# Windowed attention and a spectral filter on one core: query and key stacks kept threefold in DRAM, and the score maxima passed through DRAM

## The chip, the cores and the metric

The program runs on one core of one Trainium2 chip. The metric is the time on the device of one execution, in microseconds (us). The kernel before takes 1365.38 us, the median of three runs from 1363.18 to 1367.34. The profile is of one execution with a span of 1361.8 us between its first and its last instruction; the 3.6 us up to the median lie outside that span.

## What is computed

The input `x` has 2048 tokens of 576 features. Four steps follow one another, attention (A), spectral filter (B), A, B, each added to its input after a layer norm. The attention has 32 heads of 18 features and a window of 256 tokens.

```python
def _A_ref(x, wqkv, wo):                       # S = 2048, D = 576
    H = 32; Dh = D // H; W = 256
    qkv = transpose((x @ wqkv).reshape(B, S, 3, H, Dh), 2, 0, 3, 1, 4)
    q, k, v = qkv[0], qkv[1], qkv[2]
    scores = einsum("bhqd,bhkd->bhqk", q, k) * (Dh ** -0.5)
    mask = (idx[:, None] - idx[None, :] >= 0) & (idx[:, None] - idx[None, :] < W)
    p = softmax(where(mask, scores, -1e9))
    return transpose(einsum("bhqk,bhkd->bhqd", p, v), 0, 2, 1, 3).reshape(B, S, D) @ wo

x = x + _A_ref(_layernorm(x), A_wqkv, A_wo)
x = x + _B_ref(_layernorm(x), B_w_r, B_w_i)    # rfft2, times a weight, irfft2
x = x + _A_ref(_layernorm(x), A_wqkv, A_wo)
x = x + _B_ref(_layernorm(x), B_w_r, B_w_i)
```

## The kernel before

All the work around the change is in `layer_a`, which runs twice, once for each attention. The order of the instructions is written out by hand, and each engine and each queue of DMAs keeps the order of the program.

**Numbers in two parts.** TensorE multiplies in a reduced float format, so a float is kept as a high part and a low part, and a product is made of high times high, high times low and low times high. For a score of queries and keys this is one matmul over a stack of rows: the query stack has the features' high parts, their high parts again, and their low parts; the key stack has high, low, high. One head has 18 features, so that a stack is 54 rows. `qs` and `ks` (two buffers each) hold the stacks of one group `n` of four heads: head half `hp` 0 in partitions 0 to 53 and `hp` 1 in partitions 64 to 117, two heads (`pair`) side by side in the columns. There are NQ = 8 groups. Partition 63 (and 127) of `qs` holds minus the maximum of each query's scores, and the same partition of `ks` holds ones, so that the second score matmul subtracts the maximum.

**Projection.** `proj(i, c)` makes 128 columns of queries and keys (block `i` of 9) for a chunk `c` of 512 tokens, with 14 matmuls (L1112). ScalarE takes the high part (L1124), VectorE the low part (L1127, in `remainder`), and one DMA writes both to `qk_d` in DRAM (L1129, 512 KB): `qk_d[part, column, token]`. For blocks 0 and 1 it goes out on ScalarE's queue, for the others on SyncE's (SP). `qk_cols` sets the order of the columns: all the queries of group 0, then its keys, then group 1.

**Stacks.** `stack_load(n, c)` reads `qk_d` back. A row of 18 features with one part goes to its own 18 partitions, so a chunk of a group takes 2 (queries, keys) x 2 (`hp`) x 3 (slots of the stack) = 12 DMAs of 72 KB (L1144), nearly all on SP.

**Two score matmuls and the maxima.** `score_max` multiplies queries by keys (L1169) and takes each query's maximum (L1171) into a tile `ms[n, c]`. `m_rows(n, c)` transposes that tile (L1182), ScalarE copies it with a minus sign to `mt`, 16 rows of 128 (L1184), and four DMAs of 2 KB move it within the SBUF to row 63 or 127 of `qs` (L1189), on SP (for the first two chunks on ScalarE's queue). `exps` multiplies keys by queries with that row (L1206) and takes the exponential (L1207). `part` multiplies by the values (L1226), `norm` transposes the sums, divides and stores to `o_d` (L1251, on SP).

**The order.** `x` counts tiles of 128 tokens, 16 in each group. `opening` runs ten steps of score maxima (LEAD = 10) beside projections. `bursts` then runs 158 bursts `k`, each with three `exps` and three `score_max`, some `part`, one or two tasks out of `due` (`m_rows` or `norm`) and a few matmuls of `pj`, the projections still to be made. At the start of a burst `loads(x)` issues the stack loads (every fourth `x`, 20 tiles ahead) and the loads of values (`v_load`, once for each group, beside chunk 2 of the same group's stack). A store of a projection that ended in a burst is issued by `remainders()` in the next burst. The first `exps` that reads chunk `c` of a group is that of tile 4c-2 (tile 0 for chunk 0). Two short loops follow for the tiles from MIX = 118.

Of the kernel before, what the change touches and what calls it, by code (L numbers as in the profile page):

```python
# [632 lines left out]
NQ = 8  # L633
# [13 lines left out]
def qk_cols():  # L647
    c = []
    for n in range(NQ):
        for qk in range(2):  # L650
            for hp in range(2):
                for pair in range(2):
                    h = head_of(n, hp, pair)
                    c += [qk * D + h * DH + d for d in range(DH)]
    return np.array(c)
# [209 lines left out]
def layer_a(tc, ident, eps, bp, src, dst, wqk_d, wv_d, wo_d, dc_d, gc_d, dram, copy, wvs, second, spectral, share):  # L865
# [4 lines left out]
    qk_d = dram.tile([2, 1152, S], F32R, name="qk_d")  # L870
# [12 lines left out]
    if True:  # L883
# [192 lines left out]
        with ExitStack() as c2:  # L1076
# [21 lines left out]
            def proj(i, c, bank=0):  # L1098
# [5 lines left out]
                def mm(s, k):  # L1104
# [8 lines left out]
                    if s == len(ks) - 1:  # L1113
                        if 4 * i + c < 12:

                            sg = wp.tile([128, 4, 384], F32, tag="P", name=f"sg{i}_{c}", bufs=6)
                            sg = sg.rearrange("r a b -> r (a b)")[:, 0:1024].rearrange("r (a t) -> r a t", a=2).bitcast(F32R)
                        else:
                            sg = wp.tile([128, 2, 512], F32R, tag="sg", name=f"sg{i}_{c}", bufs=2)
                        by, rest = box["ps"], sg  # L1120
                        if second:
                            by = by.rearrange("r (n p) -> r p n", n=NT)
                            rest = sg.rearrange("r a (p n) -> r a p n", n=NT)
                        A.copy(rest[:, 0], by)  # L1124

                        def remainder():
                            V.tensor_sub(rest[:, 1], by, rest[:, 0].bitcast(F32))  # L1127

                            (nc.scalar if i < 2 else nc.sync).dma_start(qk_d[:, 128 * i:128 * i + 128, cs].rearrange("a r t -> r a t").bitcast(F32), sg.bitcast(F32))  # L1129
                        ended.append(remainder)  # L1130
# [4 lines left out]
            def stack_load(n, c):  # L1135
# [3 lines left out]
                for which, t, parts in ((0, q, (0, 0, 1)), (1, k, (0, 1, 0))):  # L1139
                    for hp in range(2):  # L1140
                        r0 = 144 * n + 72 * which + 36 * hp
                        for slot, part in enumerate(parts):
                            b = 64 * hp + 18 * slot
                            (P if which and (n == 0 and c > 1 or n == 1 and c == 0) else nc.sync).dma_start(  # L1144
                                t[b:b + 18, :, cs].bitcast(F32), qk_d[part, r0:r0 + 36, cs].rearrange("(f d) t -> d f t", f=2).bitcast(F32))
# [33 lines left out]
            def m_rows(n, c):  # L1179
# [5 lines left out]
                for hp in range(2):  # L1185
                    for pair in range(2):
                        r = (hp * 2 + pair) * 4
                        b = 64 * hp + 63
                        (nc.sync if n or c > 1 else nc.scalar).dma_start(q[b:b + 1, pair, c * 512:c * 512 + 512].rearrange("a (t q) -> a t q", t=4).bitcast(F32),  # L1189
                                          mt[r:r + 4].bitcast(F32))  # L1190
# [75 lines left out]
            done, due = 0, []  # L1266
# [16 lines left out]
            def opening():  # L1283

                n = 0
                for t in range(-LEAD, 0):
# [8 lines left out]
                    if y > 0 and y % 4 == 3:  # L1295
                        m_rows(0, y // 4)
                    yield from pj[n + 3:want]
# [12 lines left out]
            def bursts():  # L1310
# [8 lines left out]
                for k in range(-(-len(es) // 3)):  # L1319
# [40 lines left out]
                    for f, *a in tasks:  # L1360
                        f(*a)
                    for f in pj[at + early:at + n]:
# [6 lines left out]
                    due.extend(new)  # L1369
                    for x, pair, hp in e:  # L1370
# [55 lines left out]
            for t in range(MIX, NX + 2):  # L1426
# [9 lines left out]
                if MIX < y < NX - 1 and y % 4 == 3 and t != NX - 1:  # L1436
                    due.append((norm, *divmod(y // 4, 4)))
                for f, *a in due[:1]:
                    f(*a, *([True] if f is norm else []))
                    due.pop(0)  # L1440
                behind(t)
            assert not due
# [76 lines left out]
```

## Time and profile before

| what | value |
|---|---|
| time of the kernel, median of 3 runs | 1365.38 us (1363.18 to 1367.34) |
| profiled execution, span | 1361.8 us |
| busy: VectorE, ScalarE, GpSimd | 900.8, 779.3, 642.9 us |
| attention in bursts, first layer and second layer | about 128 to 443 us and 822 to 1141 us |
| read from HBM, written to HBM | 156.11 MB, 101.01 MB |

Times in the profile count from the first instruction. PE is TensorE's matmul, PEld its load of weights, DVE VectorE, ACT ScalarE, POOL GpSimd, SP SyncE, which only issues DMAs here; a q behind an engine's name is its sequencer, so that SPq L1144 is the issue of a DMA by line 1144. An issue's duration is the time for which it holds its queue, not the transfer's. `qs<-mt` is an instruction that reads `mt` and writes `qs`. A busy PE is not PE at its peak: matmuls are pipelined.

### The profile page before, as it was taken

The numbers are of one execution on the slowest core, as the hardware profiler recorded it, in microseconds if no ns is written. First come the engines' busy times: TensorE is split into PE (matmuls) and PEld (weight loads), VectorE is DVE, ScalarE is ACT, GpSimd is POOL, SyncE is SP. The second block draws the span as 40 slices with busy tenths as digits, with TensorE's granted clock in tenths as the row PEclk, the third lists the DMA queues.
The fourth block names the chain that finished last, engine by engine and source line by source line (L and its number), as shares of the span: only waits on it lengthen the run. The fifth ranks groups of instructions, "written<-read, shape, count | busy, mean of one in ns | idle before, by whom it ended". The sixth has DMA issues, their size and how long they took to land.

```text
span 1361.8 us, 33597 instructions
## 1 busy us (share of the span) xinstructions
PE 1333.3 (98%) x11351; PEld 994.7 (73%) x11351; DVE 900.8 (66%) x3060; ACT 779.3 (57%) x1966; POOL 642.9 (47%) x1154
## 2 busy tenths in 40 slices
PE   9999999999999999999999999999999999999998
PEld 8986666666665699975999975566666655898587
DVE  5418777877778366666673157777777785575755
ACT  5522777777778544543355316677777778464223
POOL 2257545555546533477221394445455458112721
PEclk9999999999999999999999999999999999999999
DMA  6756665655546547778873467566555555597875
GB/s 204 208 166 195 206 184 171 192 166 159 153 144 178 134 150 253 225 231 255 268 248 73 113 196 218 167 178 164 165 140 152 159 162 164 143 358 248 309 237 173
DMA packets 202313, 259.11 MB, mean 190 GB/s; under 512 B 104487, under 2 KB 109863, under 8 KB 201631
## 3 DMA queue, kind: packets, MB, share of 16 engines
q1 hardware_dynamic: 191439, 235.72, 57.6%
q10 hardware_dynamic: 7648, 14.96, 3.2%
q0 software_dynamic: 3056, 6.28, 1.8%
q8 instruction: 92, 1.51, 0.5%
q14 instruction: 78, 0.64, 0.1%
HBM read 156.11 MB, written 101.01 MB: 189 GB/s over the span
## 4 chain that ended last, share of the span: by engine, by line
PE 87%; DMA 5%; DVE 3%; issue 2%; ACT 2%; SPq 1%; POOL 0%; ACTq 0%; DVEq 0%; POOLq 0%
PE pj L1112 18%; PE S L1169 12%; PE U L1226 12%; PE vps L1005 8%; PE ops L800 7%; PE E L1206 6%; PE po L257 4%; PE pq L517 2%; PE p L496 2%; PE pf L257 2%; PE tpo L1240 2%; PE pi L591 2%; PE pz L295 2%; DMA qs<-mt 1%; PE tpm L1182 1%
## 5 line engine op out<-in xcount | busy, mean ns | idle before, releaser
L1171 DVE CUSTOM_DVE_ANT_0 jk<-S,mask 128x384 bf16<-128x384 f32 (+2 forms) x1024 | 490.7, 529 | 111.0 <-PE E L1206 53.7
L1207 ACT ACTIVATE P<-E 128x384 f32<-128x384 f32 (+2 forms) x1024 | 408.9, 477 | 125.6 <-PE E L1206 92.1
L1209 POOL TENSOR_SCALAR_AFFINE_SELECT P<-P 128x512 f32<-128x512 f32 x256 | 162.5, 635 | 275.7 <-ACT P L1207 257.3
L1169 PE MATMUL S<-ks,qs 63*128 63x384 f32 (+2 forms) x1024 | 269.5, 371 | 1.1 <-DVE m L1171 0.4
L1206 PE MATMUL E<-qs,ks 64*128 64x384 f32 (+2 forms) x1024 | 222.7, 372 | 4.5 <-ACT P L1207 2.7
L1169 PEld LDWEIGHTS S<-ks,qs 63*128 63x128 f32 x1024 | 140.7, 184 | 105.4 <-DVE m L1171 72.0
L1226 PE MATMUL U<-P,vq 128*19 128x128 f32 (+1 forms) x3840 | 187.8, 328 | 0.6
L1112 PE MATMUL pj<-xh,wqh 128*128 128x512 f32 x360 | 155.9, 433 | 1.5 <-DVE sg L1127 1.1
L1226 PEld LDWEIGHTS U<-P,vq 128*19 128x19 f32 x3840 | 95.9, 98 | 77.1 <-issue 24.3
L1212 POOL TENSOR_SCALAR_AFFINE_SELECT P<-P 128x512 f32<-128x512 f32 x224 | 142.2, 635 | 0.0
L1206 PEld LDWEIGHTS E<-qs,ks 64*128 64x128 f32 x1024 | 113.9, 185 | 19.7 <-ACT P L1207 9.9
L1112 PE MATMUL pj<-xh,wql 128*128 128x512 f32 x360 | 124.4, 419 | 0.0
L1112 PE MATMUL pj<-xl,wqh 128*128 128x512 f32 x288 | 122.1, 424 | 0.0
L800 PE MATMUL ops<-oroom 128*128 128x290 f32 (+1 forms) x812 | 115.4, 298 | 0.4 <-DVE ofree L846 0.2
L800 PEld LDWEIGHTS ops<-oroom 128*128 128x128 f32 x812 | 110.3, 189 | 1.1 <-DVE ofree L823 0.7
L1112 PEld LDWEIGHTS pj<-xh,wqh 128*128 128x128 f32 x360 | 67.7, 188 | 32.3 <-issue 10.6
L1171 DVE DVE_READ_ACCUMULATOR2_ANT m<- 128x1 f32 x1024 | 85.0, 83 | 0.0
L1127 DVE TENSOR_TENSOR sg<-pj,sg 128x512 fp32r<-128x512 f32 x72 | 49.5, 687 | 52.2 <-ACT sg L1124 52.2
L1124 ACT CAST sg<-pj 128x512 fp32r<-128x512 f32 x72 | 42.2, 586 | 68.8 <-PE pj L1112 51.7
L1112 PEld LDWEIGHTS pj<-xh,wql 128*128 128x128 f32 x360 | 64.3, 189 | 20.2 <-issue 10.7
L1005 PE MATMUL vps<-wvh,xh 128*128 128x288 f32 x320 | 71.4, 304 | 0.0
L1112 PEld LDWEIGHTS pj<-xl,wqh 128*128 128x128 f32 x288 | 54.3, 189 | 18.2 <-issue 11.5
(599 smaller groups left out, 2251.9 us busy)
## 6 DMA issues: line engine op xcount, KB each, us to landing
qk_d<-sg SPq DMA_DIRECT2D x56, 512.0 KB
qs<-qk_d SPq DMA_DIRECT2D x384, 72.0 KB
ks<-qk_d SPq DMA_DIRECT2D x348, 72.0 KB
v_d<-vt SPq DMA_DIRECT2D x32, 304.0 KB
vq<-v_d SPq DMA_DIRECT2D x16, 608.0 KB
wt<-in_w SPq DMA_DIRECT2D x16, 580.0 KB
ofree<-x SPq DMA_DIRECT2D x16, 580.0 KB
x<-ofree SPq DMA_DIRECT2D x32, 290.0 KB
```

What stands on the lines that cost most here:

```text
L257: T.matmul(ps[:, c, 0:NF], tail[r] if si == 4 else hl_(si), dcs[b // 2][r, b % 2], start=mi == si == 0, stop=si == 4)
L800: self.nc.tensor.matmul(self.ps[u][n][:, 0:self.n], x, self.w[p][:, (2 * wk + n) * self.n:(2 * wk + n + 1) * self.n], start=first and i == ...
L1005: T.matmul(ps[:, n, 0:288], xT(xk, c), w[:, wk, n * 288:(n + 1) * 288], start=i == 0, stop=i == len(ks) - 1)
L1112: T.matmul(box["ps"].rearrange("r (n p) -> r n p", n=NT) if second else box["ps"], w[:, wk], x, start=s == 0, stop=s == len(ks) - 1)
L1127: V.tensor_sub(rest[:, 1], by, rest[:, 0].bitcast(F32))
L1169: T.matmul(ps[:, 0:N], q[b:b + 63, pair, i * 128:i * 128 + 128], k[b:b + 63, pair, lo:hi], start=True, stop=True)
L1171: V.tensor_tensor_reduce(out=jk[:, 0:N], in0=ps[:, 0:N], in1=mask[:, 384 - N:384], scale=1.0, scalar=-3e38, op0=ALU.add, op1=ALU.max, accu ...
L1206: T.matmul(ps[:, 0:nq], k[b:b + 64, pair, j * 128:j * 128 + 128], q[b:b + 64, pair, j * 128:j * 128 + nq], start=True, stop=True)
L1207: A.activation(p[:, hl_, 0:nq], ps[:, 0:nq], AF.Exp, scale=SC)
L1209: P.affine_select(out=p[:, :, 0:128], in_=p[:, :, 0:128], pattern=[[0, 4], [1, 128]], compare_op=ALU.is_ge, fill=0.0, base=0, channel_mult ...
L1212: P.affine_select(out=p[:, :, 256:384], in_=p[:, :, 256:384], pattern=[[0, 4], [-1, 128]], compare_op=ALU.is_gt, fill=0.0, base=0, channel ...
L1226: T.matmul(U[32 * h:32 * h + 19, (q0 % 4) * 128:(q0 % 4) * 128 + 128 * (q1 - q0)], vts[n][:, j, h], pt[n, j][:, h, (q0 - j) * 128:(q1 - j) ...
```

## The change

Each feature gets three rows in DRAM, in the order in which a stack wants them. `qk_d` becomes `[2, 576, 3, S]`: queries or keys, feature, slot, token. `qk_cols` now puts 64 queries and 64 keys of the same features into each block of 128. A projection's store becomes four DMAs: for queries the high part to slots 0 and 1 (one DMA that reads it twice, 256 KB) and the low part to slot 2 (128 KB), for keys the high part to slots 0 and 2 and the low part to slot 1. A stack of one head half is then 54 rows that lie side by side in DRAM, and a chunk of a group takes 4 DMAs of 216 KB. The 54 partitions now go feature by feature with the slots inside, instead of slot by slot; the matmul sums over them all the same.

The maxima go through a new DRAM tile `m_d`: `m_rows` writes `mt` to it with one DMA of 8 KB, and a new function `m_load` reads it into both rows of `qs` with one more. `m_load` runs at the end of the burst that is two after that of `m_rows` (in the opening one step later, in the last loop one tile later). Both use the queue that the four DMAs had.

```diff
@@ -645,14 +645,8 @@
     return 4 * n + 2 * hp + pair
 
 def qk_cols():
-    c = []
-    for n in range(NQ):
-        for qk in range(2):
-            for hp in range(2):
-                for pair in range(2):
-                    h = head_of(n, hp, pair)
-                    c += [qk * D + h * DH + d for d in range(DH)]
-    return np.array(c)
+    c = np.array([head_of(n, hp, pair) * DH + d for n in range(NQ) for hp in range(2) for pair in range(2) for d in range(DH)])
+    return np.stack([c, D + c]).reshape(2, 9, 64).transpose(1, 0, 2).reshape(-1)
 
 def lay_qkv(wqkv):
     w3 = lay_w3(wqkv[:, qk_cols()])
@@ -867,7 +861,8 @@
     nc = tc.nc
     V, A, T, P = nc.vector, nc.scalar, nc.tensor, nc.gpsimd
     SC = float(DH) ** -0.5
-    qk_d = dram.tile([2, 1152, S], F32R, name="qk_d")
+    qk_d = dram.tile([2, D, 3, S], F32R, name="qk_d")
+    m_d = dram.tile([NQ, 4, 16, 128], F32R, name="m_d")
     v_d = dram.tile([NQ, S, 76] if second else [NQ, 128, NT, 76], F32, name="v_d")
 
     o_d = dram.tile([S, 448], F32, name="o_d")
@@ -1126,7 +1121,12 @@
                         def remainder():
                             V.tensor_sub(rest[:, 1], by, rest[:, 0].bitcast(F32))
 
-                            (nc.scalar if i < 2 else nc.sync).dma_start(qk_d[:, 128 * i:128 * i + 128, cs].rearrange("a r t -> r a t").bitcast(F32), sg.bitcast(F32))
+                            e = nc.scalar if i < 2 else nc.sync
+                            for which, high, low in ((0, slice(0, 2), 2), (1, slice(0, 3, 2), 1)):
+                                d = qk_d[which, 64 * i:64 * i + 64].bitcast(F32)
+                                s = sg[64 * which:64 * which + 64].bitcast(F32)
+                                e.dma_start(d[:, high, cs], s[:, 0:1].to_broadcast([64, 2, 512]))
+                                e.dma_start(d[:, low, cs], s[:, 1])
                         ended.append(remainder)
                 return [lambda s=s, k=k: mm(s, k) for s, k in enumerate(ks)]
 
@@ -1136,13 +1136,11 @@
 
                 q, k = qs[n % 2], ks_[n % 2]
                 cs = slice(c * 512, c * 512 + 512)
-                for which, t, parts in ((0, q, (0, 0, 1)), (1, k, (0, 1, 0))):
+                for which, t in ((0, q), (1, k)):
                     for hp in range(2):
-                        r0 = 144 * n + 72 * which + 36 * hp
-                        for slot, part in enumerate(parts):
-                            b = 64 * hp + 18 * slot
-                            (P if which and (n == 0 and c > 1 or n == 1 and c == 0) else nc.sync).dma_start(
-                                t[b:b + 18, :, cs].bitcast(F32), qk_d[part, r0:r0 + 36, cs].rearrange("(f d) t -> d f t", f=2).bitcast(F32))
+                        r0 = 72 * n + 36 * hp
+                        (P if which and (n == 0 and c > 1 or n == 1 and c == 0) else nc.sync).dma_start(
+                            t[64 * hp:64 * hp + 54, :, cs].bitcast(F32), qk_d[which, r0:r0 + 36, :, cs].rearrange("(a d) s t -> (d s) a t", a=2).bitcast(F32))
 
             def v_load(n):
                 v = wp.tile([128, NT, 4, 19], F32, tag="vq", name=f"vq{n}", bufs=2)
@@ -1182,12 +1180,13 @@
                 T.transpose(tp[0:16, 0], ms[n, c].rearrange("p a b t -> p (a b t)"), ident)
                 mt = wp.tile([16, 128], F32R, tag="mt", name=f"mt{n}_{c}", bufs=2)
                 A.activation(mt, tp[0:16, 0], AF.Copy, scale=-1.0)
-                for hp in range(2):
-                    for pair in range(2):
-                        r = (hp * 2 + pair) * 4
-                        b = 64 * hp + 63
-                        (nc.sync if n or c > 1 else nc.scalar).dma_start(q[b:b + 1, pair, c * 512:c * 512 + 512].rearrange("a (t q) -> a t q", t=4).bitcast(F32),
-                                          mt[r:r + 4].bitcast(F32))
+                m_queue(n, c).dma_start(m_d[n, c].bitcast(F32), mt.bitcast(F32))
+
+            def m_queue(n, c):
+                return nc.sync if n or c > 1 else nc.scalar
+
+            def m_load(n, c):
+                m_queue(n, c).dma_start(qs[n % 2][63:128:64, :, c * 512:c * 512 + 512].bitcast(F32), m_d[n, c].rearrange("(a p t) q -> a p (t q)", a=2, p=2).bitcast(F32))
 
             pt = {}
 
@@ -1263,7 +1262,7 @@
             NX = NQ * NT
             LEAD = 10
             pj = [f for i in range(2, 9) for c in range(4) for f in proj(i, c, c % 2 if i == 2 else c == 0 and i == 3)]
-            done, due = 0, []
+            done, due, steps = 0, [], {}
 
             MIX = 118
 
@@ -1294,6 +1293,8 @@
                     yield from pj[n:n + 3]
                     if y > 0 and y % 4 == 3:
                         m_rows(0, y // 4)
+                    if y > 0 and y % 4 == 0:
+                        m_load(0, y // 4 - 1)
                     yield from pj[n + 3:want]
                     n = want
 
@@ -1359,6 +1360,8 @@
                         yield f
                     for f, *a in tasks:
                         f(*a)
+                        if f is m_rows:
+                            steps.setdefault(k + 2, []).append((m_load, *a))
                     for f in pj[at + early:at + n]:
                         yield f
                     at += n
@@ -1367,6 +1370,8 @@
                     if (3 * k) // 4 + LEAD - 1 < full and full % 4 == 3:
                         new.append((m_rows, *divmod(full // 4, 4)))
                     due.extend(new)
+                    for f, *a in steps.pop(k, ()):
+                        f(*a)
                     for x, pair, hp in e:
                         if pair == hp == 1:
                             behind(x)
@@ -1435,11 +1440,15 @@
                 y = t - 3 if t == NX - 2 else t - 4
                 if MIX < y < NX - 1 and y % 4 == 3 and t != NX - 1:
                     due.append((norm, *divmod(y // 4, 4)))
+                for f, *a in [z for k in sorted(steps) for z in steps.pop(k)]:
+                    f(*a)
                 for f, *a in due[:1]:
                     f(*a, *([True] if f is norm else []))
                     due.pop(0)
+                    if f is m_rows:
+                        steps.setdefault(0, []).append((m_load, *a))
                 behind(t)
-            assert not due
+            assert not due and not steps
             def bank(tag, name):
                 return pp.tile([128, 512], F32, tag=tag, name=name, bufs=1 if tag == "pj" else 3)
 
```

## The prediction

> **What bounds the kernel now.** I read the page first, then TensorE's waits, the DMA issues by line, SP's own queue in order of time, and the chain.
>
> ```profile
> PE 1333.3 (98%) x11351; PEld 994.7 (73%) x11351; DVE 900.8 (66%) x3060; ACT 779.3 (57%) x1966; POOL 642.9 (47%) x1154
> q1 hardware_dynamic: 191439, 235.72, 57.6%
> PE 87%; DMA 5%; DVE 3%; issue 2%; ACT 2%; SPq 1%; POOL 0%; ACTq 0%; DVEq 0%; POOLq 0%
> ```
>
> TensorE is busy 98% of the span and holds 87% of the chain, so a wait costs time where TensorE itself waits. The list of its waits says how much of that DMAs cause:
>
> ```profile
> PE E L1206 <- ACT P L1207: 2.7, 7, 0.5
> ...
> PE E L1206 <- DMA qs<-mt: 1.8, 2, 1.5
> ...
> PE S L1169 <- DMA qs<-qk_d: 0.3, 1, 0.3
> ```
>
> Columns: us in total, times, longest. Only 2.1 us of the whole run hang on the DMAs that the change touches. So nothing much can be won by making them quicker; what counts is whether one of them becomes late. The nearest to that are the maxima. The PE rows that follow are the first `exps` of chunk 1 of group 1 and of chunk 2 of group 2, the ACT rows the ends of their `m_rows`, the DMA rows the chain:
>
> ```profile
> 169.68 0.27 ACT L1184 ACTIVATE mt<-tpm 16x128 fp32r<-16x128 f32 x1
> 178.34 0.93 PE L1206 MATMUL E<-qs,ks 64*128 64x384 f32 x3 [0.30 <-DMA qs<-mt]
> 225.54 0.25 ACT L1184 ACTIVATE mt<-tpm 16x128 fp32r<-16x128 f32 x1
> 231.66 0.62 PE L1206 MATMUL E<-qs,ks 64*128 64x384 f32 x3
> 125.91 2.33 DMA qs<-mt
> 174.34 3.87 DMA qs<-mt
> 870.10 4.26 DMA qs<-mt
> ```
>
> From the end of `mt` (169.95) to the matmul that needs it are 8.4 us, of which 0.3 are already a wait: a budget of 8.1 us, where five bursts lie between. For the other chunk (225.79; the matmul is the third of its three, at about 231.9) four bursts lie between, 6.1 us. A small DMA lands 2.33 us after its issue when little is ahead of it, and 3.87 or 4.26 us where it stands behind other loads. SP's queue shows what stands there:
>
> ```profile
> 162.45 2.28 SPq L1144 DMA_DIRECT2D qs<-qk_d  x6
> 164.78 2.56 SPq L1144 DMA_DIRECT2D ks<-qk_d  x6
> 167.44 2.81 SPq L1144 DMA_DIRECT2D qs<-qk_d  x6
> 170.32 2.23 SPq L1144 DMA_DIRECT2D ks<-qk_d  x6
> 172.65 0.38 SPq L1129 DMA_DIRECT2D qk_d<-sg  x1
> 173.35 0.38 SPq L1251 DMA_DIRECT2D o_d<-o  x1
> 174.34 2.48 SPq L1189 DMA_DIRECT2D qs<-mt  x4
> ```
>
> `mt` was ready at 169.95, its first DMA went out at 174.34 behind two sets of stack loads, and TensorE waited at 178.34. In the second layer the same place (870.10) costs TensorE 1.5 us. That is a late maximum's price: TensorE stands still, for its queue keeps order.
>
> **What goes.** The issues by line (columns: ns min/median/max, first and last start):
>
> ```profile
> L1144 SPq DMA_DIRECT2D qs<-qk_d x384: 265/321/770, 89.6 to 1115.7; - x192
> L1144 SPq DMA_DIRECT2D ks<-qk_d x348: 264/320/1312, 93.7 to 1118.1; - x174
> L1144 POOL DMA_DIRECT2D ks<-qk_d x36: 577/587/808, 114.5 to 823.7; - x36
> L1189 SPq DMA_DIRECT2D qs<-mt x240: 572/573/2832, 138.6 to 1145.8; - x120
> L1129 SPq DMA_DIRECT2D qk_d<-sg x56: 360/387/2451, 124.6 to 1111.0; - x56
> L1129 ACTq DMA_DIRECT2D qk_d<-sg x16: 366/366/397, 84.4 to 799.3; - x16
> ```
>
> Stack loads on SP fall from 732 to 244 (488 x 0.32 = 156 us of SP's time), on POOL from 36 to 12 (24 x 0.59 = 14 us). The maxima's 240 SP issues of 0.573 become 120 of 0.3 to 0.57: 69 to 100 us less. Stores grow from 56 to 224 on SP (168 x 0.387 = 65 us more) and from 16 to 64 on ACT (48 x 0.366 = 18 us more). SP gains 160 to 190 us, and its backlog of 4.4 us (169.95 to 174.34) should vanish. None of it is on the path except the 2.1 us above. The price if that cover is gone is the next part.
>
> **What comes, away from the maxima.** The rows are ACT's copies of two blocks in turn, its issues for chunk 1's maxima, and the last chunk of group 7:
>
> ```profile
> 87.92 0.59 ACT L1124 CAST sg<-pj 128x512 fp32r<-128x512 f32 x1 [2.50 <-PE pj L1112]
> 91.09 0.59 ACT L1124 CAST sg<-pj 128x512 fp32r<-128x512 f32 x1 [2.58 <-PE pj L1112]
> 125.29 2.50 ACTq L1189 DMA_DIRECT2D qs<-mt  x4
> 445.96 0.25 ACT L1184 ACTIVATE mt<-tpm 16x128 fp32r<-16x128 f32 x1
> 449.89 0.90 PE L1206 MATMUL E<-qs,ks 64*128 64x384 f32 x4
> ```
>
> Each store writes 768 instead of 512 KB: 72 x 0.26 = 19 MB more beside 259. In the blocks ahead of the opening ACT issues 4 x 0.37 = 1.5 us for each; a block comes every 3.2 us and ACT's copy takes 0.6, so it fits. In the opening `m_load` waits on ACT's queue until `m_d` has landed, with ACT's copy of the last projection and the first exponentials behind it. Before, four issues held ACT there for 2.5 us, about as long; between 0 and 1.5 us for each layer, I take 0.5. In the last loop the chunk has 3.7 to 4.0 us (446.21 to a matmul of the group at 449.89); two landings of 2.3 make it about 0.5 late in each layer. In return the opening's loads come sooner; I take 1 us off for each layer, up to 1.5.
>
> **What comes, for the maxima.** One transfer becomes two, with a wait of SP between. Two idle landings (4.7 us) fit both budgets. But `m_load` stands at the end of a burst at whose beginning `loads` has issued that period's whole set of stack loads, and often a store and the values, all behind `m_rows` and ahead of `m_load` on SP. Before, the four DMAs of `mt` went out ahead of them. This period shows it:
>
> ```profile
> 225.82 2.53 SPq L1189 DMA_DIRECT2D qs<-mt  x4
> 228.45 0.39 SPq L1129 DMA_DIRECT2D qk_d<-sg  x1
> 228.94 2.47 SPq L1144 DMA_DIRECT2D qs<-qk_d  x6
> 231.45 4.21 SPq L1144 DMA_DIRECT2D ks<-qk_d  x6
> 235.76 0.77 SPq L1152 DMA_DIRECT2D vq<-v_d  x1
> 227.40 0.69 DVE L1127 TENSOR_TENSOR sg<-pj,sg 128x512 fp32r<-128x512 f32 x1
> ```
>
> After the change the order is `m_d`, store (ready at 228.09, when VectorE is done: 2.3 us behind `mt`), four stack loads, values, `m_load`, and the matmul wants it at 231.9. Packets ahead on a queue hold a small DMA up, as 3.87 and 4.26 against 2.33 show, so I let `m_load` wait for all of them.
>
> How long each takes to drain. A set of stack loads: the 24 loads from 162.45 to 172.55 took 10.1 us, 5.05 for twelve, an upper end, since issue may have held them; by q1's row (57.6% of 16 x 1361.8 us for 235.72 MB is 53.2 us for one MB on one engine) 0.885 MB over sixteen engines take 2.9, the lower end. I take 4.3: near the set that was seen, less something for eight DMAs fewer. A store of 0.786 MB over sixteen engines: 2.6 (at the least the 1.7 of today's 0.524 MB). Values, 0.623 MB: 2.0, at the least 1.0.
>
> The Trainium skill speaks here against the change: by "DMA: Bandwidth & Descriptors", section "Why a DMA increments its semaphore by 16 and not by 1", a DMA runs on the largest number of engines up to 16 that divides its outermost dimension, 9 for 18 rows and again 9 for 54, so the wider load is spread no wider. No view here shows the number of engines. With its 27 GiB/s for an engine, an estimate from that page's figure, set, store and values would drain in 3.4, 1.7 and 1.3 us, and the sum below would be 53 us instead of 107.
>
> The order written in `bursts` gives four kinds among the 20 chunks of a layer whose `m_load` has a set ahead of it and whose budget is 6.1 or 8.1 (chunk 0 of each group has over two bursts more and stays in time). 2.3 is the landing of `m_load` itself:
> - set alone (0.4 for the issue of `m_d` + 4.3 + 2.3 = 7.0): late by 0.9 at three chunks of four bursts, in time at four of five: 2.7.
> - set and values (9.0): 0.9 at two, 2.9 at one: 4.7.
> - store and set (2.3 + 2.6 + 4.3 + 2.3 = 11.5): 3.4 at five, 5.4 at one: 22.4.
> - store, set and values (13.5): 5.4 at three, 7.4 at one: 23.6.
>
> That is 53.4 for a layer, 107 for both. TensorE has few other waits that a standstill could absorb, so I count all of it. With the 2.1 us that go, 1 + 1 that come and 2 that the openings give back: 107 - 2 = 105. On the profiled execution's 1361.8 this is 1467; the median of the runs lies 3.6 above that span: **1470 us**. With the lower drains the kinds give 0, 0.5, 8.6 and 10.4, so 39 and 1402; with 5.05 for a set 5.0, 7.0, 26.9 and 26.6, so 131 and 1494.
>
> **The rivals.**
> - *The relief of SP decides* (faster). If `m_load` lands within its budget everywhere, the 2.1 us go and the openings give up to 3: about 1361. It decides once store and set drain within 8.1 - 2.3 - 2.3 = 3.5 us, half of what I sum. The skill's same page, section "Rules for kernel authors", advises to merge many small transfers into a large one; by that rule this is the outcome, and the 160 us of SP's time agree, but TensorE's waits do not need them.
> - *The small load is not held* (no change). Then only issues count: with a store 2.3 + 4 x 0.39 + 4 x 0.33 + 2.3 = 7.5, late at the two chunks of four bursts by 1.4 and 1.8, so 6 for both layers against 4 to 5 given back: 1367. Against it stand 3.87 and 4.26.
> - *Held, but the drains are shorter than my lower ends*, as the engines overlap reads and writes: 1374 to 1402.
> - *The store's parts wait for one another*, because slots 0 and 2 lie around slot 1: SP would stand for a landing of a store, 4.88 in the chain's row below, at ten chunks of a layer: 98 more, 1568.
>
> ```profile
> 830.71 4.88 DMA qk_d<-sg
> ```
>
> **How the numbers follow.** Forecast 0.62 (its own range 1402 to 1494), shorter drains 0.15, between 1494 and 1512 0.03, the store's waits 0.05, no change 0.08, faster 0.07. The range from 1374 to 1512 holds 0.80. Slower by over 0.3% (4 us, about what a measurement of this kernel can tell from no change): 0.85; within 0.3%: 0.08; faster: 0.07.
>
> **What would show it.** TensorE's waits should list L1206 waiting for the DMA of `qs<-m_d` some thirty times, 3 us each, in both layers, longest where store, set and values meet (chunk 2 of groups 0, 2, 4 and 6); SP's queue should have `m_load` right behind four loads of 216 KB; issues on SP should fall by 440. I am wrong if L1206's wait stays under 10 us in total, if `m_load` lands some 2.3 us after its issue behind a set, or if SP stands at the second DMA of a store.

## The result and the profile after

The changed kernel takes 1619.3 us (median of four runs, 1617.37 to 1623.9) against 1366.1 for the kernel before on the same chip: a ratio of 1.186, 95% interval 1.183 to 1.188. That is slower, as forecast, but the forecast loss was 105 us, the measured one 253, and the time lies outside the range. The profiled execution has a span of 1617.9 us, 256.1 more than before.

From the page of the changed kernel come the busy times, the granted clock in 40 slices and the chain by engine:

```profile
PE 1417.3 (88%) x11351; PEld 1045.1 (65%) x11351; DVE 904.1 (56%) x3060; ACT 787.2 (49%) x1966; POOL 631.6 (39%) x1130
...
PEclk9989788799899899999999988987897998999999
...
PE 61%; DMA 25%; SPq 4%; DVE 3%; issue 3%; ACT 2%; POOL 1%; ACTq 0%; DVEq 0%; POOLq 0%
```

TensorE does the same 11351 matmuls and is busy 84.0 us longer with them (1417.3 against 1333.3). Outside them it stands 200.6 us (1617.9 - 1417.3) against 28.5: 172.1 more. So a third of the loss is not waiting at all. DMAs now hold 25% of the chain, against 5%. Its waits (us in total, times, longest) say what it stands for:

```profile
PE E L1205 <- DMA qs<-m_d: 157.5, 34, 8.7
PE E L1205 <- ACT P L1206: 9.8, 6, 4.3
PE pj L1107 <- DVE sg L1122: 9.2, 8, 2.6
```

Thirty-four waits for the maxima's load, 4.6 us each, are 157.5 of the 172.1. Here is one of them, chunk 2 of group 0. First SP's queue, then TensorE, then the chain's row for the load:

```profile
150.31 0.33 SPq L1183 DMA_DIRECT2D m_d<-mt  x1
150.93 0.59 SPq L1128 DMA_DIRECT2D qk_d<-sg  x1
152.84 0.45 SPq L1129 DMA_DIRECT2D qk_d<-sg  x1
153.34 1.49 SPq L1128 DMA_DIRECT2D qk_d<-sg  x1
154.89 0.60 SPq L1129 DMA_DIRECT2D qk_d<-sg  x1
155.53 1.29 SPq L1142 DMA_DIRECT2D qs<-qk_d  x2
156.87 0.76 SPq L1142 DMA_DIRECT2D ks<-qk_d  x2
157.67 0.72 SPq L1150 DMA_DIRECT2D vq<-v_d  x1
158.43 0.61 SPq L1189 DMA_DIRECT2D qs<-m_d  x1
```

```profile
158.47 0.32 PE L1167 MATMUL S<-ks,qs 63*128 63x128 f32 x1
166.84 0.98 PE L1205 MATMUL E<-qs,ks 64*128 64x384 f32 x3 [8.05 <-DMA qs<-m_d]
```

```profile
158.43 8.28 DMA qs<-m_d
```

`m_d` goes out at once. Then come four store DMAs (the second, a low part, waits for VectorE until 152.84), four stack loads and the values; `m_load` is issued 8.1 us after `mt` and lands 8.3 us after that. TensorE stands 8.05 us. What happens to its clock is seen in windows around that wait (window, its length, PE busy and matmuls, PEld, DVE, ACT, POOL, granted clock, DMA share, GB/s):

```profile
150.00:158.00 8.00, 7.86 (x76) 4.82 (x78) 6.68 (x26) 6.32 (x16) 4.77 (x7) 1.00 0.50 112
158.50:166.80 8.30, 0.29 (x5) 0.15 (x1) 0.30 (x2) 0.58 (x1) 1.10 (x2) 0.74 0.82 198
166.80:174.00 7.20, 7.16 (x54) 4.37 (x54) 2.48 (x12) 3.54 (x9) 1.22 (x2) 0.59 0.20 46
174.00:179.80 5.80, 5.80 (x59) 3.65 (x57) 4.34 (x19) 4.20 (x11) 3.11 (x5) 1.00 0.73 168
```

After the wait the clock is at 0.59 for 7 us and TensorE, fully busy, makes 54 matmuls where it made 76 in 8 us before it; then the clock is 1.00 again. The trace has 39 stretches of half clock, 239 us in all, each 3.4, 6.8 or 10.2 us long, against one at the very end before. TensorE is busy for 177 us of them. Outside them its matmuls take as long as in the kernel before (`exps` of 384 columns 382 ns in both kernels on average, projections 423 against 425); those that touch them take 604 and 672. So the longer matmuls are the lower clock's. The Trainium skill, "TensorE: Matmul & The Clock Gate", section "HAM oscillation — how this bites in real kernels", says that a wait for a DMA that fills an activity window of some 3.4 us halves the array's clock and that the next work starts slow. The trace agrees, in steps of 3.4 us.

By stages (between the starts of the first projection of the loop, of the first `exps` and of that of tile 118, both layers): blocks and opening grew by 9.7 and 8.9 us, the bursts by 121.0 and 117.2, everything else together by -0.7.

### The profile page after: what moved, and what is told of

Its sections match the earlier page's. It is cut to its first block, busy times and chain, and to the rows that moved or that the text cites. A ratio compares the mean times of both kernels' runs of the same rounds, so it can differ in the third digit from the quotient of the medians.

```text
span 1617.9 us, 33055 instructions
## 1 busy us (share of the span) xinstructions
PE 1417.3 (88%) x11351; PEld 1045.1 (65%) x11351; DVE 904.1 (56%) x3060; ACT 787.2 (49%) x1966; POOL 631.6 (39%) x1130
## 4 chain that ended last, share of the span: by engine, by line
PE 61%; DMA 25%; SPq 4%; DVE 3%; issue 3%; ACT 2%; POOL 1%; ACTq 0%; DVEq 0%; POOLq 0%
DMA qs<-m_d 14%; PE pj L1107 10%; PE S L1167 7%; PE vps L1000 7%; PE U L1225 6%; PE ops L794 6%; PE E L1205 5%; DMA qk_d<-sg 4%; PE po L257 3%; PE pq L517 2%; PE tpo L1239 2%; SPq L1142 2%; PE p L496 2%; PE pf L257 2%; PE pi L591 2%
## 5 line engine op out<-in xcount | busy, mean ns | idle before, releaser
L1205 PE MATMUL E<-qs,ks 64*128 64x384 f32 (+2 forms) x1024 | 244.0, 403 | 168.9 <-DMA qs<-m_d 157.5
L1167 PE MATMUL S<-ks,qs 63*128 63x384 f32 (+2 forms) x1024 | 288.1, 394 | 2.8 <-DVE m L1169 2.5
L1205 PEld LDWEIGHTS E<-qs,ks 64*128 64x128 f32 x1024 | 123.1, 202 | 189.2 <-issue 163.8
L1167 PEld LDWEIGHTS S<-ks,qs 63*128 63x128 f32 x1024 | 155.0, 203 | 116.5 <-DVE m L1169 69.7
L1107 PE MATMUL pj<-xh,wqh 128*128 128x512 f32 x360 | 170.5, 474 | 9.8 <-DVE sg L1122 9.2
L1107 PE MATMUL pj<-xh,wql 128*128 128x512 f32 x360 | 140.9, 468 | 0.0
L1107 PE MATMUL pj<-xl,wqh 128*128 128x512 f32 x288 | 133.2, 462 | 0.0
L1107 PEld LDWEIGHTS pj<-xh,wqh 128*128 128x128 f32 x360 | 74.6, 207 | 46.7 <-issue 16.9
L1245 POOL TENSOR_TENSOR o<-ts,rc 128x288 f32<-128x288 f32 x62 | 41.8, 675 | 131.4 <-DVE rc L1243 130.3
L1107 PEld LDWEIGHTS pj<-xh,wql 128*128 128x128 f32 x360 | 73.6, 216 | 24.4 <-issue 14.6
```

Source lines behind the costliest of these rows:

```text
L1107: T.matmul(box["ps"].rearrange("r (n p) -> r n p", n=NT) if second else box["ps"], w[:, wk], x, start=s == 0, stop=s == len(ks) - 1)
L1167: T.matmul(ps[:, 0:N], q[b:b + 63, pair, i * 128:i * 128 + 128], k[b:b + 63, pair, lo:hi], start=True, stop=True)
L1205: T.matmul(ps[:, 0:nq], k[b:b + 64, pair, j * 128:j * 128 + 128], q[b:b + 64, pair, j * 128:j * 128 + nq], start=True, stop=True)
```

## The experiments

Theory A at the start: the maxima's load is late because it stands on SP's queue behind the store and the set, and nothing else of the change costs much. The rivals: B, the wide stores and 54-row loads themselves; C, two landings in a row are too long wherever they stand. For the clock, D (it falls because TensorE stands) against E. The kernel before ran beside each group at 1364 to 1366 us; the ratios are to it.

**One half of the change without the other.** First the maxima straight from `mt`:

```diff
-                m_queue(n, c).dma_start(m_d[n, c].bitcast(F32), mt.bitcast(F32))
+                for hp in range(2):
+                    for pair in range(2):
...
+                        (nc.sync if n or c > 1 else nc.scalar).dma_start(q[b:b + 1, pair, c * 512:c * 512 + 512].rearrange("a (t q) -> a t q", t=4).bitcast(F32),
+                                          mt[r:r + 4].bitcast(F32))
```

> Changed kernel, but m_rows sends the maxima straight from mt into the stacks in four DMAs, as before; m_d and m_load are gone, the threefold stacks and their stores stay. Theory A (the small load is late because it stands on SP's queue behind the store and the set of its burst; nothing else of the change costs much): TensorE's waits for the maxima fall under 10 us, granted clock 0.995 or more, 1358 to 1374 us. Rival B (the wide stores and the 54-row loads occupy the DMA engines so that whatever small transfer there is comes late, or TensorE waits for the stacks themselves): over 1400. Rival C (two landings one after the other are too long, wherever the load stands): 1358 to 1374 as well.

Measured: 1404.38 us, ratio 1.028 (1.025 to 1.031), clock 0.988. Its waits:

```profile
PE pj L1106 <- DVE sg L1121: 11.7, 8, 3.3
PE E L1203 <- DMA qs<-mt: 8.8, 8, 2.0
```

The maxima's wait falls to 8.8 us, and with it go 215 of the 253 us. But 39 us stay, outside what A allowed and just inside what B did (over 1400): the stores and stacks cost something by themselves. Then the other half, an edit of the kernel before, with `qk_d`, its store and the twelve loads left as they were:

```diff
+                m_queue(n, c).dma_start(m_d[n, c].bitcast(F32), mt.bitcast(F32))
...
+                            steps.setdefault(k + 2, []).append((m_load, *a))
```

> Kernel before, with only the second half of the change: m_d is written by m_rows and m_load follows two bursts later; the stacks load as before, in twelve DMAs of 18 rows, the store is the one DMA of before. Theory A: the order alone does it, so m_load stands behind twelve loads of 0.32 us of issue each and their drain; from mt to the landing 10 to 14 us against the 14 to 16 of the changed kernel, some 30 waits of 2 to 4 us, with the clock's part 1420 to 1560. Rival B: little is late without the wide transfers, 1366 to 1400. Rival C: 1450 or more, with waits at nearly all of the 64 chunks.

Measured: 1596.21 us, ratio 1.169 (1.165 to 1.172), clock 0.937.

```profile
PE E L1208 <- DMA qs<-m_d: 147.5, 41, 9.0
```

Nearly the whole loss comes from the maxima's way alone, 231 us, more than A's range and inside C's, though 41 waits are not C's nearly all of 64. The 54-row loads are not needed for it. From `mt` to the landing it takes 9.5 us behind a set and 15.2 behind store, set and values, against 9.2 and 15.9 in the changed kernel, but the time is made differently: here `m_load` is issued late, behind twelve issues, and lands 2.9 us later; there it is issued sooner and lands 4.6 us later behind a set (means from the trace's issues and landings).

**Where the load stands.** At once behind `m_d`:

```diff
                 m_queue(n, c).dma_start(m_d[n, c].bitcast(F32), mt.bitcast(F32))
+                m_load(n, c)
```

> Changed kernel, with m_load issued directly behind the write of m_d, ahead of the store and the set of the next bursts. Theory A: SP stands some 1.4 us for m_d's landing at each of 64 chunks, the load lands about 2.3 us after its issue, 4.5 us after mt, inside every budget of 6.1 us or more: waits for qs<-m_d under 15 us in total, clock 0.99 or more, 1360 to 1385 us. Rival B: the wide transfers of the burst before still hold it, 1420 to 1550. Rival C: the detour stays too long, over 1450.

Measured: 1513.01 us, ratio 1.108 (1.106 to 1.110). A missed by over 100 us; the time lies in the ranges of B and C. SP's waits and TensorE's, and chain rows of one chunk, show why:

```profile
SPq L1190 <- DMA m_d<-mt: 245.9, 60, 9.3
```

```profile
PE E L1206 <- DMA qs<-m_d: 76.0, 23, 7.7
```

```profile
162.09 8.39 DMA m_d<-mt
170.54 1.92 DMA qs<-m_d
```

The second trip takes 1.9 us (2.0 on average); it is now the first that lands late (8.4 us here), behind the set of the bursts before, as B has it, and SP stands for it 4.1 us a time while its next loads and stores wait, too. So either trip can be caught by the bulk, and making SP wait moves the lateness on. Next, `m_load` at the start of burst k + 2 instead of its end, so that only a store can be ahead:

```diff
+                    for f, *a in steps.pop(k, ()):
+                        f(*a)
                     for x, pair, hp in e:
                         if pair == hp == 0:
                             loads(x)
...
-                    for f, *a in steps.pop(k, ()):
-                        f(*a)
```

> Changed kernel, with m_load at the start of the burst k + 2, ahead of that burst's stack loads and values, still behind a store issued in the burst before. Theory A: without the set ahead, the landing comes 6 to 10 us after mt where a store stands ahead and 4 to 5 where none does: waits for qs<-m_d of 30 to 70 us in place of 157, 1450 to 1530. Rival H (the store, not the set, is what holds it): 1570 or more.

Measured: 1448.85 us, ratio 1.062 (1.058 to 1.067), just under A's range.

```profile
PE E L1205 <- DMA qs<-m_d: 38.1, 16, 5.3
```

A load issued before the set instead of behind it wins 170 us: the set and the values are what holds it most, and H falls. The 38.1 us left stem mostly from the first trip: `m_d` itself now takes 4.1 us to land on average, against 1.9 in the changed kernel. So C isn't refuted altogether: at none of the places tried on SP's queue is the detour as cheap as the direct way, and the best is 44 us above direct maxima. Then the same place as in the change, but on ScalarE's queue:

```diff
-                m_queue(n, c).dma_start(qs[n % 2][63:128:64, :, c * 512:c * 512 + 512].bitcast(F32), m_d[n, c].rearrange("(a p t) q -> a p (t q)", a=2, p=2).bitcast(F32))
+                nc.scalar.dma_start(qs[n % 2][63:128:64, :, c * 512:c * 512 + 512].bitcast(F32), m_d[n, c].rearrange("(a p t) q -> a p (t q)", a=2, p=2).bitcast(F32))
```

> Changed kernel, but every m_load is issued by ScalarE, on its queue, at the same place of the program; m_d is still written on SP's queue. Theory A (what holds the small load is the order of one queue): it lands 2 to 2.5 us after its issue, the waits for qs<-m_d fall under 25 us, and what is left over the kernel before is the 39 us that the changed kernel with direct maxima kept: 1395 to 1440. Rival F (the DMA engines are what is full, so a second queue helps nothing): landings of 5 us and more, over 1500. Rival G (ScalarE stands at the issue until a transfer some places ahead has landed, and the exponentials with it): 1440 to 1500, with waits for ACT in place of those for the DMA.

Measured: 1482.01 us, ratio 1.088 (1.083 to 1.092).

```profile
PE E L1205 <- DMA qs<-m_d: 34.8, 16, 4.5
PE E L1205 <- ACT P L1206: 26.2, 16, 4.8
```

Two cases must be told apart. In the first a set is on its way. SP's row of its values, and the chain's row of the load issued on ScalarE's queue 1.3 us later:

```profile
203.66 0.35 SPq L1150 DMA_DIRECT2D vq<-v_d  x1
```

```profile
204.92 7.21 DMA qs<-m_d
```

Such a load lands as late from the other queue: 4.8 us after its issue behind a set, 6.6 behind set and values, against 4.6 and 6.4 on SP's own queue. Here the traffic on the DMA engines holds it, not the order of one queue, as F says. The Trainium skill, "DMA: Bandwidth & Descriptors", section "Issuing engines are not separate DMA queues", says that DMAs run on the same 16 DMA engines and interleave, whichever engine issues them; the trace agrees in this case.

In the second case a store stands ahead of the set, and SP with it, until VectorE is done. Here is chunk 2 of group 0 again: ScalarE's issue, the store that SP stood at, and the start of the set:

```profile
152.91 0.50 ACTq L1189 DMA_DIRECT2D qs<-m_d  x1
153.08 0.46 SPq L1129 DMA_DIRECT2D qk_d<-sg  x1
155.75 1.29 SPq L1142 DMA_DIRECT2D qs<-qk_d  x2
```

ScalarE isn't held up by SP's issues, so the load leaves ahead of the set (at 16 of the 20 such chunks) and lands 2.0 us later. From `mt` to the landing it takes 8.4 us at the chunks with store and set and 5.2 at those with values, too, in place of 13.4 and 15.9, and TensorE's waits at these 20 chunks fall from 119.2 to 3.5 us. That is how this run beats the changed kernel by 137 us: A is right that the order on SP's queue is a large part, F is right that a second queue can't help once the set is under way, and the time lands in G's range with 26.2 us of waits for ScalarE, against 9.8.

**Nine engines.** Each stack load cut in two:

```diff
+                        for u, v in ((0, 48), (48, 54)):
...
-                            t[64 * hp:64 * hp + 54, :, cs].bitcast(F32), qk_d[which, r0:r0 + 36, :, cs].rearrange("(a d) s t -> (d s) a t", a=2).bitcast(F32))
+                                t[64 * hp + u:64 * hp + v, :, cs].bitcast(F32), qk_d[which, r0:r0 + 36, :, cs].rearrange("(a d) s t -> (d s) a t", a=2)[u:v].bitcast(F32))
```

> Changed kernel, each stack load cut into one of 48 rows and one of 6, so that most packets of a set spread over sixteen engines instead of nine; eight issues a set instead of four. Theory K (nine engines are why a set drains slowly): the set drains 1.5 to 3 us sooner, four issues cost 1.4 us back: waits for qs<-m_d 90 to 145, 1540 to 1605. Rival L (the number of engines does not matter behind a store and beside the values): 1610 to 1670, for the issues alone.

Measured: 1586.86 us, ratio 1.165 (1.160 to 1.170), as K said.

```profile
PE E L1206 <- DMA qs<-m_d: 134.1, 36, 8.3
```

Behind a set alone `m_load` now lands 2.9 us after its issue instead of 4.6, but is issued 1.0 us later, for the four more issues. In the trace of the changed kernel mostly nine packets of 2 KB are under way while nothing but 54-row loads runs, so the nine engines are real, and they are a part of the set's size, not most of the loss.

**The clock.** TensorE kept busy in its waits with matmuls that are overwritten:

```diff
+                if hp == pair == 0 and (j == 0 or j % 4 == 2):
+                    for _ in range(FILL.get((n, (j + 2) // 4), 0)):
+                        T.matmul(ps[:, 0:nq], k[b:b + 63, pair, j * 128:j * 128 + 128], q[b:b + 63, pair, j * 128:j * 128 + nq], start=True, stop=True)
```

> Changed kernel, with 441 matmuls in each layer that are computed and overwritten, put ahead of the first exps matmul of 19 chunks (between 3 and 48 of them, about the measured wait divided by 0.18 us), so that TensorE works while it would stand. The transfers are unchanged. Theory D (the granted clock of 0.927 and TensorE's 84 us of longer matmuls come from standing still): the clock rises to 0.97 or more; the load lands as late as before, so part of what is won becomes waiting: 1535 to 1595 us. Rival E (the clock is lowered by something else, or the longer matmuls come from other traffic): clock 0.92 to 0.94 and 1612 to 1640 us.

Measured: 1573.65 us, ratio 1.151 (1.146 to 1.156), clock 0.984. D holds: 882 useless matmuls make the kernel 46 us faster. The landings are as late as in the changed kernel (15.9 us after `mt` in the worst kind, both), so the 46 are taken to be the part of the 84 that doesn't turn into waiting; 11 stretches of half clock, 52 us, are left.

**The 39 us of the other half.** Twelve loads of 18 rows out of the threefold tensor, stores as changed, maxima direct:

```diff
+                        for slot in range(3):
+                            b = 64 * hp + 18 * slot
...
+                                t[b:b + 18, :, cs].bitcast(F32), qk_d[which, r0:r0 + 36, slot, cs].rearrange("(a d) t -> d a t", a=2).bitcast(F32))
```

> Changed kernel with direct maxima, its threefold tensor and its four-DMA stores kept, but each half stack loaded again in three DMAs of 18 rows, one for each slot, twelve a set as before. Theory I (what direct maxima lost, 39 us, comes from the stores): 1390 to 1415. Rival J (it comes from the loads of 54 rows): 1362 to 1380.

Measured: 1470.15 us, ratio 1.077 (1.073 to 1.080).

```profile
PE E L1205 <- DMA qs<-mt: 45.7, 21, 5.0
```

J falls, and I's number is missed, too: with the new stores, the old loads are 66 us worse than the 54-row ones. So the merged loads are a gain, and the stores cost about 105 us beside twelve loads; beside four, stores and loads together cost some 40. Then only the store cut in two, in the kernel before:

```diff
-                            (nc.scalar if i < 2 else nc.sync).dma_start(qk_d[:, 128 * i:128 * i + 128, cs].rearrange("a r t -> r a t").bitcast(F32), sg.bitcast(F32))
+                            for r in (0, 64):
+                                (nc.scalar if i < 2 else nc.sync).dma_start(qk_d[:, 128 * i + r:128 * i + r + 64, cs].rearrange("a r t -> r a t").bitcast(F32), sg[r:r + 64].bitcast(F32))
```

> Kernel before, its one store of 128 rows of sg cut into two DMAs of 64 rows each; bytes and places are the same, there is one issue more for each of 72 stores. Theory O (a DMA that reads or writes only 64 rows of SBUF moves its 2 KB packets slower): the packets of the stores take some 147 ns, as in the changed kernel, against 86 before, and a store drains in 2.4 us instead of 1.4; 1364 to 1376 us. Rival P (the slower packets come from the threefold write or from the same row read twice): packets of 84 to 90 ns, 1362 to 1372 us.

Measured: 1393.12 us, ratio 1.020 (1.017 to 1.023), outside both ranges.

```profile
894.01 1.33 SPq L1130 DMA_DIRECT2D qk_d<-sg  x2
895.44 0.63 SPq L1252 DMA_DIRECT2D o_d<-o  x1
896.17 3.19 SPq L1190 DMA_DIRECT2D qs<-mt  x4
```

```profile
PE E L1207 <- DMA qs<-mt: 13.2, 9, 4.9
```

Same bytes, same places, one DMA more for each store: 28 us. Two issues hold SP 1.33 us in place of 0.38, the maxima behind them go out a microsecond later, and nine waits, 13.2 us in all, appear with a clock of 0.988. So the kernel before had little margin on this queue. As to O and P, neither is as stated: while nothing else is under way, over half of these packets take 140 to 175 ns, but a third 84 to 88. Where one such store runs quite alone, the first half's packets take about 147 ns and the second half's 84, so the 64 rows alone don't make a packet slow. How the 28 us divide between the issue and these packets is not shown. Then the openings:

```diff
-                            e = nc.scalar if i < 2 else nc.sync
+                            e = nc.sync
```

> Changed kernel with direct maxima, and the stores of the first two blocks of each layer issued by SyncE, too, not by ScalarE. Theory M (about half of the 39 us arises in the openings, because ScalarE stands at its 32 store issues for transfers still to land, TensorE then waits for the projections' PSUM, and the clock falls): the waits of pj for sg fall from 11.7 us to under 3, blocks and opening take 53 us a layer instead of 61: 1378 to 1392. Rival N (SyncE's queue is as full there, the stores only come later and the first stacks with them): 1398 to 1420.

Measured: 1412.15 us, ratio 1.034 (1.030 to 1.038): N, not M.

```profile
PE E L1203 <- DMA qs<-mt: 18.1, 6, 5.5
PE S L1166 <- DMA qs<-qk_d: 15.6, 4, 6.5
```

The waits of `pj` are gone, as M said, but TensorE waits for the first stacks and maxima instead; blocks and opening still take 60.7 us in the first layer. Last, an attempt to make the stores wide, in two forms with direct maxima. The first makes three DMAs of all 128 rows of `sg`, with views of `qk_d` of different strides:

```diff
+                            for r0, apart, part in ((0, 1728, 0), (1, 1729, 0), (2, 1727, 1)):
+                                d = qk_f[r0:r0 + 2 * apart].rearrange("(w r) t -> w r t", w=2)[:, 192 * i:192 * i + 190:3, cs]
+                                e.dma_start(d.bitcast(F32), sg[:, part].bitcast(F32))
```

> Changed kernel with direct maxima, and the store made of three DMAs that each read all 128 rows of sg (slot 0 of q and k; slot 1 of q with slot 2 of k; slot 2 of q with slot 1 of k) instead of four that read 64 rows. Bytes in DRAM and their places are the same. Theory I (the 39 us of direct maxima come from the stores: packets of 147 ns against 86 before, four issues of 0.6 us on ScalarE in the openings): packets return to 84 to 90 ns, TensorE's waits for sg vanish, 1363 to 1382. Rival J (they come from the loads of 54 rows): 1394 to 1410.

Measured: 2591.11 us, ratio 1.899 (1.894 to 1.904). It can't tell I from J, for two other things happened:

```profile
SPq L1127 <- DMA qk_d<-sg: 899.2, 112, 12.1
```

SP stood at the second and third DMA of each of its 56 stores until the one ahead had landed, and each store moved with two packets under way at a time. The second form shifts the rows so that the high slots are plain views, and the parts don't wait for one another; its companion adds the cut of the loads:

```diff
+                            high = qk_d[:, 1:1729].rearrange("w (r s) t -> w r s t", s=3)[:, 64 * i:64 * i + 64, :, cs].bitcast(F32)
+                            for s in range(2):
+                                e.dma_start(high[:, :, s], sg[:, 0].bitcast(F32))
+                            for w in range(2):
+                                e.dma_start(low[w], sg[64 * w:64 * w + 64, 1].bitcast(F32))
```

> Changed kernel with direct maxima, its store rearranged: a query's three rows in DRAM are low, high, high and a key's high, high, low, so that each high slot of both is one DMA of all 128 rows of sg; the two low slots stay DMAs of 64 rows. Four DMAs, the same bytes, 54-row loads. Theory I (the half-width packets are what direct maxima lost to): a store drains in 2.5 us in place of 3.5, 1366 to 1392 us. Rival Q (four issues in place of one, and ScalarE's and SyncE's standing for earlier transfers at them, are what was lost; width does not matter): 1396 to 1412.

> The same with each stack load cut into 48 and 6 rows, spread over sixteen engines instead of nine, at four more issues a set. Theory K (the spread makes a set drain sooner, and what is behind it come sooner): 5 to 15 us under the run without the cut. Rival Q (issues and earlier transfers at them count): 5 to 25 us over it.

Measured: 1910.32 us, ratio 1.398 (1.394 to 1.402), and 1900.19, ratio 1.392 (1.388 to 1.395). Chain rows of the first:

```profile
101.30 20.61 DMA qk_d<-sg
126.49 14.66 DMA qk_d<-sg
```

A store that took 4.6 us to land in the chain of direct maxima takes 15 to 20. Its packets need only 84 ns each, but two at a time. The destination's outermost dimension is 2 (queries, keys). By the Trainium skill's rule that the prediction cites ("DMA: Bandwidth & Descriptors", section "Why a DMA increments its semaphore by 16 and not by 1") a DMA then runs on two engines; the trace agrees. Whether full-width stores over sixteen engines would win the 39 us back was not tried. The companion is 10 us faster, as K said there, which tells little at this level.

## Why the prediction was wrong in size and right in kind

| kind of chunk, `m_load` behind | chunks | `mt` to landing, forecast | measured mean | waits forecast, both layers | measured |
|---|---|---|---|---|---|
| set | 14 | 7.0 | 9.2 | 5.4 | 19.5 |
| set, values | 6 | 9.0 | 10.9 | 9.4 | 17.9 |
| store, set | 12 | 11.5 | 13.4 | 44.8 | 58.4 |
| store, set, values | 8 | 13.5 | 15.9 | 47.2 | 60.8 |

(Measured from the trace's issues and landings; all in us. The other 0.9 us of the 157.5 fell at a chunk 0.)

- **The mechanism was right.** The four kinds and their counts are there, 34 waits instead of some thirty, the longest where store, set and values meet, in both layers; issues on SP fell by the 440 forecast. Its test, the set taken from ahead of the load, cut the waits from 157.5 to 38.1.
- **The set's term was mis-sized.** Every kind is 1.9 to 2.4 us over its forecast, with the same gap whether a store or values stand ahead: the store's share (4.2 us against 4.5) and the values' (1.7 to 2.5 against 2.0) were about right, and what was put at 4.3 for the set was about 6.4. The waits came to 157.5 us instead of 107: 51 of the missing 148. Not all of the 6.4 is the set's drain. At 8 of the 14 chunks of the first kind nothing but the set stands between, and the landing comes 8.4 us after `mt`, which makes the set 5.7. The 5.05 us taken as its upper end came from the pace at which twelve small loads were issued, and is no bound for four large ones on nine engines. At the other six the forecast overlooked what else SP issues there. At two it is a load of weights (L890): landings of 11.4 and 12.4 us, and 10.1 of the kind's 19.5 us of waits. At four SP stands 3.8 to 5.4 us for GpSimd at a store of `norm`, here from 357.04 to 361.01:

```profile
354.97 2.07 SPq L1142 DMA_DIRECT2D ks<-qk_d  x2
361.01 0.39 SPq L1250 DMA_DIRECT2D o_d<-o  x1
361.50 0.55 SPq L1189 DMA_DIRECT2D qs<-m_d  x1
```

The load then lands some 2.0 us after its issue, the set being through; TensorE did not wait at these four.
- **The price of a wait was taken as its length.** "I count all of it" left out the clock: 84.0 us of longer matmuls, the largest error. The kernel before showed no idle stretch of TensorE over 2.2 us, so its trace couldn't show what longer ones do. The run with filled waits shows the cause; at least 46 us of the 84 are lost to it alone. With only the maxima's detour, a microsecond of waiting for the maxima went with some 1.6 of loss (231 us for 147.5).
- **The stores were not free.** Cost at about 1 us away from the maxima, the other half of the change loses 39 us by itself. The forecast saw 1.5 us of issue on ScalarE in a stage where a block comes every 3.2 us. But the issues also stand for earlier transfers, and in the opening `m_load` holds ScalarE. Its rows, and TensorE's behind them:

```profile
134.72 0.36 ACTq L1183 DMA_DIRECT2D m_d<-mt  x1
140.18 0.53 ACTq L1189 DMA_DIRECT2D qs<-m_d  x1
140.75 0.58 ACT L1119 CAST sg<-pj 128x512 fp32r<-128x512 f32 x1 [6.06 <-DMA m_d<-mt]
```

```profile
141.78 0.53 PE L1205 MATMUL E<-qs,ks 64*128 64x384 f32 x1 [3.56 <-ACT P L1206]
```

ScalarE stands 5.1 us for `m_d`'s landing, where the forecast took 0.5 us for each layer (up to 1.5). With the stores' part, blocks and opening lose 9 us a layer instead of giving half a microsecond back. The 0.5 us forecast for the last chunk of each layer did not come: TensorE waits for none of group 7's maxima.
- **The relief of SP** was rightly called worth no more than the 2.1 us it could save in the kernel before; no run here is faster than that kernel. But the relief isn't worthless: once the stores are heavier, four loads instead of twelve are worth 66 us.
- **The other rivals.** That the small load is not held is refuted by the rows of the changed kernel above. That the parts of a store wait for one another did not happen in the changed kernel (SP's stop at 152.84 is VectorE's low part), but in the run with views of different strides it did, 112 times. What is left of the 256 us after 157.5 and 84.0 is 14.6, mostly 7.1 more for ScalarE's exponentials and 8.1 more for `sg` in the blocks.

What stays open is how the 39 us divide between the stores' slower packets, their number of issues and ScalarE's part in the openings: none was undone alone without a new wait. By stages, blocks and openings grew by 22.3 us in the profiled execution of direct maxima, and the bursts by 18.4.

## What to carry to other kernels

A small transfer that the critical engine waits for must go out ahead of the bulk, in one trip. A second trip through DRAM is cheap (1.9 us) only where nothing is on the way. What decides is whether it leaves ahead of the bulk. A second queue helps as far as it lets the transfer leave sooner (137 us here), and not once the bulk is under way, which is on the same DMA engines. When you price a wait on TensorE, add the clock that falls behind it, and when a queue's budget is already used up in the profile, price every added issue ahead of the urgent one.

## What the runs showed of the hardware

- In the changed kernel the stores' 2 KB packets, out of 64 rows of SBUF, take 146 ns (median of those seen while no load was under way), against 86 ns for the full 128 rows before, with sixteen under way in both. The Trainium skill, "SBUF — State Buffer", section "Door 1: The DMA port swizzle (why `[64,N]` ≈ `[32,N]`)", has rows 0 to 63 on half of the SBUF's DMA ports. The changed kernel's packets agree with that; the run with the store in two halves, whose second half moved at 84 ns, does not, so the cause stays open.
- A broadcast store issue of two slots holds SP 0.60 us in the median (0.55 for one slot), against 0.39 for the one store before.
- A rewritten store whose destination has an outermost dimension of 2 had two packets under way at a time and took 15 to 20 us to land.
